# Load durations in the planner, the staging depth of the weights, and a rule of order for float32 matmuls

## The chip, the cores and the metric

The kernel runs on one core of a Trainium2 chip. The metric is the device time of one execution in microseconds, as the median of several runs. PE (TensorE) multiplies matrices, DVE (VectorE), ACT (ScalarE) and POOL (GpSimd) work element by element, SP (SyncE) issues the DMAs here. Each engine works through its own instructions in the written order.

## The reference

A dynamic convolution is followed by two feed-forward layers. There are 8192 tokens of 192 features.

```python
# 1. convolution: softmax over 7 taps for each token and each of 8 heads, then a weighted sum
w = exp(weight_gen - max); w = w / (sum(w) + 1e-9)
x = einsum('bshk,bskhg->bshg', w, last_7_tokens(x))      # (8192, 192)
# 2. a layer with a rational activation, 192 -> 2048 -> 192
h = x @ w_in
P = a0 + a1*h + a2*h**2 + a3*h**3
Q = 1 + abs(b0)*abs(h) + abs(b1)*h**2
x = (P / (Q + 1e-6)) @ w_out
# 3. a layer with hard swish, 192 -> 2048 -> 192
h = x @ w_in2
out = (h * clip(h + 3, 0, 6) / 6) @ w_out2
```

The four weight matrices come as float64 (x and the gate weights as float32), 12.6 MB in all, so the kernel decodes their bit patterns to float32 itself.

## The kernel before

**Tiling.** The tokens are cut into 32 blocks of 256 (a block is also a unit, `u`). The first layer works a block in four slots (`sl`), each with 4 of the 16 groups of 128 hidden features: 1024 columns. So there are 128 slots. The convolution loads x and the gate weights in 16 chunks (`load_chunk`, two units each, 945 to 960 KB of x and 112 KB of gate weights).

**First layer, per slot.** in1 (PE, L281) makes h in one of two PSUM buffers `h1`; for accuracy each product is five float32r matmuls of 256 columns, with weights and x split in a high and a low part. The activation then goes back and forth between ACT (L310 to L353), POOL (L329, L366, L377) and DVE (L333, L337, L358, L370) and ends in `ghi` and `glo`. `dve_d` (L370) is the last reader of `h1`, so in1 of a slot waits for dve_d of the slot two before. out1 (PE, L397 to L401) adds the slot to `y1`, of which there is one buffer.

**Second layer, per unit.** mid_y, mid_f and the steps around them turn y1 into the next input. in2 (L281 with win1, eight steps `q`), act_r2 (L419) and dve_g2 (L424) make g; out2 (L438, four parts of 16 matmuls in full float32, 128x192) makes the output, and evac stores it. The xT transposes (L206, L207) and mid_f (L250) are full float32 as well; all other matmuls are float32r.

**Weights.** 28 jobs load a piece of a weight each: "in" pieces of 512 KB, "pair" pieces (two halves, 512 KB together), "o1" and "o2" pieces of 384 KB. SP loads the float64 words to a staging tile `st` (ring of ST tiles), ACT decodes (`low` L490 and `scale` L484), DVE joins (L496) and sets the sign (L503), which frees the staging tile; then ACT makes the high part (L510) and POOL the low one (L511). The second layer's tiles are in memory that is free only after all jobs (`late`).

**Order.** The order on every engine is written by a planner at build time, `plan()`. Each operation has an engine, a cost, a due time `prio`, operations that it comes after, and rings of buffers that it takes from. The planner repeatedly picks the operation with the smallest rank: the earliest time at which it could start, plus a penalty for the choice of engine, plus KP times what its due time is ahead of the oldest open one's by more than WIN; ties go to the earlier due time. The multiplies of the convolution (L171) and the low parts (L511) may go to POOL or, with a handicap in us (CP and PEN), to DVE. So a cost that is wrong in the plan changes no instruction, but their order. Due times of the first layer grow by T for each slot; the constants from CH to UM set the offsets, LP how much earlier a job's load is due than its decode, XQ the same for a chunk.

SP's queue in the start, by the due times: pair 0, chunk 0, "in" piece 0, the coefficients, chunk 1, then the other jobs in their order. The planner counts 1.46 us for a 512 KB load, three quarters of that for 384 KB, and 3.1 us for a chunk, and 2.2 us more until the data is there.

Of the kernel before, what the change touches and what calls it, by code (L numbers as in the profile page):

```python
# [19 lines left out]
def kernel(  # L20
# [28 lines left out]
    BV = [n // 2 for n in BL]  # L49
# [52 lines left out]
    wgt = {}  # L102
    wk = {}

    def load_chunk(c):
        g = two.tile([P, CT * H, K], F32, tag="wg", name="wg")
        nc.sync.dma_start(
            out=g.rearrange("p (t h) k -> p t (h k)", h=H), in_=wgf[:, c * CT : (c + 1) * CT, :]
        )
        t = two.tile([P, ROWS, D], F32, tag="x", name="x")  # L110
        first = c * CT - (K - 1)
        neg = max(0, -first)
        segs = [(0, P)]
        if neg:
            segs = [(b * S // R + 1, (b + 1) * S // R) for b in range(B)]
            for b in range(B):
                p = b * S // R
                nc.gpsimd.memset(t[p : p + 1, 0:neg, :], 0.0)
                nc.sync.dma_start(
                    out=t[p : p + 1, neg:, :], in_=xf[None, b * S : b * S + ROWS - neg, :]  # L120
                )
        for p0, p1 in segs:
            src = bass.AP(
                tensor=xf.tensor,
                offset=xf.offset + (first + p0 * R) * D,
                ap=[[R * D, p1 - p0], [1, ROWS * D]],
            )
            nc.sync.dma_start(out=t[p0:p1].rearrange("p r d -> p (r d)"), in_=src)
        xch[c] = t
        wgt[c] = g  # L130

    def softmax_a(c):
        g = wgt[c]
# [313 lines left out]
        nc.sync.dma_start(out=of[:, u * 2 : u * 2 + 2, :], in_=o)  # L447

    CW = 512
    ST = 4  # L450

    def load_rows(dst, src):
        srcs = src if isinstance(src, list) else [src]
# [127 lines left out]
                    l(eng)  # L581

    G2 = 11
    T = 9.094
    CH = 5.027
    KP = 0.221
    XP = 17
    LP = 43.011
    LOADP = {(0, "load"): -100.0, (1, "load"): -80.0}
    WIN = 29  # L590
    PEN = 1.976
    CP = 3
    JP0 = 0.189
    JPT = 1.514
    HOLD = 6
    URG = 4.005
    UR = 17.898
    UG = 15.269
    SM = 1.345
    CV = 3.0  # L600
    XTP = 2.0
    XQ = 7.596
    I2 = 2.702
    SPR = 0.483
    O2 = 3.176
    OS = 3.771
    O1 = 1.491
    UM = 1.45
    ops = {}

    def op(key, eng, cost, prio, emit, after=(), take=(), lat=0.15):
# [5 lines left out]
    def add(name, eng, cost, prio, fn, *a, after=(), take=(), lat=0.15):  # L617
        op((name,) + a, eng, cost, prio, lambda *e: fn(*a, *e), after, take, lat)
# [9 lines left out]
    for n, key in enumerate(order):  # L628
# [10 lines left out]
            )  # L639

        flex = (("POOL", 1.25 * sz, 0.0), ("DVE", 0.62 * sz, PEN))
        step("load", "SP", 1.46 * sz, None, [("st", ST, [("job", key, "sign")])] if f64 else wf, 2.2)
        if f64:
            step("low", "ACT", 0.55 * sz, "load")
            step("scale", "ACT", 0.55 * sz, "load", [("s", NSB, [("job", key, "sign")])])
# [8 lines left out]
    TU = [S0[b] * T - (4 * (BV[b] - 1 - v) + XTP) * T for b, v in UB]  # L654
    for c in range(NCH):
        t = TU[2 * c] - CV * T + 1.9
        add("load", "SP", 3.1, t - XQ * T if c else -90.0, load_chunk, c, lat=2.2, take=[
            ("x", 2, [("conv_mul", 2 * c + 1, 1)]), ("wg", 2, [("softmax_b", c)]),
        ])
        add("softmax_a", "DVE", 0.75, t - SM * T + 2.85, softmax_a, c, after=[("load", c)])  # L660
        add("softmax_e", "ACT", 0.28, t - SM * T + 4.1, softmax_e, c, after=[("softmax_a", c)])
        add("softmax_b", "DVE", 1.5, t - SM * T + T + 6.6, softmax_b, c, after=[("softmax_e", c)],
            take=[("wk", 2, [("conv_mul", 2 * c + 1, 1)])])
    for u, (b, v) in enumerate(UB):
        t = TU[u]
        for i in range(2):
            flex = (("POOL", 2.6, 0.0), ("DVE", 1.6, CP))
            add("conv_mul", flex, 0, t + (2 * i - CV) * T + 1.9, conv_mul, u, i,
                after=[("load", u // 2), ("softmax_b", u // 2)],
                take=[("prod", 1, [("conv_sum", u, i, 1)])])  # L670
            for z in range(2):
                prev = [("conv_sum", u, i, 0)] if z else [("conv_sum", u, 0, 1)] if i else []
                add("conv_sum", "DVE", 1.33, t + (2 * i + z + 1 - CV) * T + 1.9, conv_sum, u, i, z,
                    after=[("conv_mul", u, i)] + prev,
                    take=[("xc", 2, [("xT", u)])] if i + z == 0 else [])
# [6 lines left out]
    for b in range(len(BL)):  # L682
        sl = S0[b] + NF // BF[b] - 1
        t = (sl + 2) * T
# [66 lines left out]
    def coeffs():  # L751
# [4 lines left out]
    op(("bab",), "ACT", 0.2, -1.0,  # L756
       lambda: nc.scalar.activation(out=bab, in_=bcol, func=AF.Abs), [("coeffs",)])

    def plan():
        free = {e: 0.0 for e in ("PE", "ACT", "DVE", "POOL", "SP")}  # L760
        end, rings, users, wait = {}, {}, {}, {}
# [15 lines left out]
        for o in sorted(ops.values(), key=lambda o: -o["prio"]):  # L777
            for f, *_ in o["choice"]:
                todo[f].append(o)
        seq = []  # L780
        while len(seq) < len(ops):
            best = None
            for e, rs in ready.items():
# [4 lines left out]
                for o, cost, pen in rs:  # L788
                    at = max([free[e]] + [end[k] for k in o["after"]])
                    for name, depth, _ in o["take"]:  # L790
# [4 lines left out]
                        if len(ring) >= depth:  # L795
                            for k in ring[-depth]:
                                at = max(at, end.get(k, float("inf")))
                    rank = (at + pen + KP * max(0.0, o["prio"] - cur - WIN), o["prio"])
                    if at < float("inf") and (pick is None or rank < pick[:2]):
                        pick = (*rank, at, e, cost, o)  # L800
# [2 lines left out]
            _, _, at, e, cost, o = best  # L803
            for f, *c in o["choice"]:
                ready[f].remove((o, *c))
            free[e] = at + cost
            end[o["key"]] = at + cost + o["lat"]
            for name, depth, rel in o["take"]:
# [53 lines left out]
```

## Time and profile before

| what | value |
|---|---|
| median of 3 runs | 1397.72 us (1397.65 to 1398.44) |
| the profiled execution, its own time | 1398.85 us |
| its span, first to last instruction | 1397.0 us |
| mean granted TensorE clock | 0.986 |
| PE busy | 1300.9 us, 93% |
| DVE, ACT, POOL busy | 1109.3, 1052.6, 1105.4 us |
| DMA queue q1 | 15656 packets, 36.44 MB |

Busy shares are of the whole span. Matmuls are pipelined and their ends modelled, so matmul times are best read from start to start. In a row of a timeline, xN means that N like instructions are merged, and the bracket says how long the engine was idle before it and what ended that.

### The profile page before, as it was taken

The numbers are of one execution on the slowest core, as the hardware profiler recorded it, in microseconds if no ns is written. First come the engines' busy times: TensorE is split into PE (matmuls) and PEld (weight loads), VectorE is DVE, ScalarE is ACT, GpSimd is POOL, SyncE is SP. The second block draws the span as 40 slices with busy tenths as digits, with TensorE's granted clock in tenths as the row PEclk, the third lists the DMA queues.
The fourth block names the chain that finished last, engine by engine and source line by source line (L and its number), as shares of the span: only waits on it lengthen the run. The fifth ranks groups of instructions, "written<-read, shape, count | busy, mean of one in ns | idle before, by whom it ended". The sixth has DMA issues, their size and how long they took to land.

```text
span 1397.0 us, 24025 instructions
## 1 busy us (share of the span) xinstructions
PE 1300.9 (93%) x9920; PEld 1292.0 (92%) x9920; DVE 1109.3 (79%) x1144; ACT 1052.6 (75%) x1326; POOL 1105.4 (79%) x492
## 2 busy tenths in 40 slices
PE   0468999999999999999999999999999999999998
PEld 0458999999999999999999999999999999999998
DVE  4988878788787878878788887878888787887762
ACT  4898777777877777787777778777778877777871
POOL 4898888878788887878878787887878888788670
PEclk9789999999999999999999999999999999999999
DMA  7530010000101000010100001010010100000000
GB/s 186 156 117 30 7 38 6 11 29 7 38 7 38 7 10 29 7 38 7 39 7 7 33 7 38 7 38 7 1 38 7 38 7 7 7 0 7 7 7 12
DMA packets 15765, 37.97 MB, mean 27 GB/s; under 512 B 1832, under 2 KB 12072, under 8 KB 15656
## 3 DMA queue, kind: packets, MB, share of 16 engines
q1 hardware_dynamic: 15656, 36.44, 8.4%
q8 instruction: 78, 1.28, 0.4%
q14 instruction: 31, 0.25, 0.1%
HBM read 30.14 MB, written 6.29 MB: 26 GB/s over the span
## 4 chain that ended last, share of the span: by engine, by line
PE 82%; DVE 6%; ACT 4%; issue 3%; DMA 2%; POOL 2%; SPq 0%; DVEq 0%; POOLq 0%
PE h L281 38%; PE y L438 24%; PE y L400 4%; PE y L401 4%; PE y L398 4%; PE y L399 4%; PE y L397 4%; DVE xc L186 2%; DMA st<-in_moe_w_in_dram 2%; DVE w L370 1%; DVE ghi L358 1%; ACT r L349 1%; ACT r L344 1%; PE yf L250 1%; DMA acol<-in_moe_a_dram 1%
## 5 line engine op out<-in xcount | busy, mean ns | idle before, releaser
L366 POOL TENSOR_TENSOR w<-w,ghi 128x1024 f32<-128x1024 f32 x128 | 308.0, 2406 | 162.4 <-DVE ghi L358 162.3
L438 PE MATMUL y<-wo,g 128*128 128x192 f32 x2048 | 353.4, 326 | 0.0
L329 POOL TENSOR_TENSOR w<-w,u 128x1024 f32<-128x1024 f32 x128 | 308.4, 2410 | 38.8 <-ACT w L315 38.5
L377 POOL TENSOR_TENSOR glo<-w,r 128x1024 fp32r<-128x1024 f32 x128 | 308.0, 2406 | 33.3 <-DVE w L370 18.0
L438 PEld LDWEIGHTS y<-wo,g 128*128 128x128 f32 x2048 | 331.1, 190 | 0.0
L281 PE MATMUL h<-xh,wst 128*128 128x256 f32 x1024 | 292.6, 286 | 0.0
L281 PE MATMUL h<-xl,wst 128*128 128x256 f32 x1024 | 292.3, 285 | 0.1
L358 DVE SCALAR_TENSOR_TENSOR ghi<-h,acol,r 128x1024 fp32r<-128x1024 f32 x128 | 163.7, 1279 | 103.5 <-ACT r L349 103.4
L344 ACT ACTIVATE r<-w 128x1024 f32<-128x1024 f32 x128 | 135.1, 1056 | 117.0 <-POOL w L329 116.7
L419 ACT ACTIVATE r<-h 128x512 f32<-128x512 f32 x256 | 153.3, 599 | 89.3 <-PE h L281 75.8
L333 DVE TENSOR_TENSOR l<-h,l 128x1024 f32<-128x1024 f32 x128 | 156.4, 1222 | 65.3 <-ACT l L322 64.8
L281 PE MATMUL h<-xh,win0hi 128*128 128x256 f32 x512 | 159.1, 311 | 48.5 <-DVE w L370 47.8
L281 PEld LDWEIGHTS h<-xl,wst 128*128 128x128 f32 x1024 | 199.2, 194 | 0.3 <-DVE xl L264 0.3
L281 PEld LDWEIGHTS h<-xh,wst 128*128 128x128 f32 x1024 | 199.0, 194 | 0.1
L424 DVE SCALAR_TENSOR_TENSOR g<-r,h 128x512 f32<-128x512 f32 x256 | 171.6, 680 | 24.6 <-ACT r L419 24.6
L186 DVE TENSOR_REDUCE xc<-prod 128x96 f32<-128x672 f32 x128 | 174.4, 1372 | 20.6 <-POOL prod L171 20.6
L370 DVE SCALAR_TENSOR_TENSOR w<-h,acol,w 128x1024 f32<-128x1024 f32 x128 | 163.7, 1279 | 22.5 <-POOL w L366 20.4
L310 ACT ACTIVATE u<-h 128x1024 f32<-128x1024 f32 x128 | 130.7, 1021 | 53.0 <-PE h L281 52.6
L171 POOL TENSOR_TENSOR prod<-x,wk 128x1344 f32<-128x1344 f32 x64 | 158.1, 2470 | 11.6 <-DVE wk L150 8.0
L337 DVE SCALAR_TENSOR_TENSOR h<-l,acol,h 128x1024 f32<-128x1024 f32 x128 | 164.1, 1282 | 0.1
L315 ACT ACTIVATE w<-u,bab 128x1024 f32<-128x1024 f32 x128 | 159.3, 1244 | 0.0
L397 PE MATMUL y<-ghi,wo1h 128*128 128x256 f32 x512 | 156.1, 305 | 0.0
(71 smaller groups left out, 3256.1 us busy)
## 6 DMA issues: line engine op xcount, KB each, us to landing
x<-in_x_dram SPq DMA_DIRECT2D x14, 960.0 KB, 4.7
st<-in_moe_w_out_dram SPq DMA_DIRECT2D x16, 384.0 KB, 3.6
out_dram<-osb SPq DMA_DIRECT2D x32, 192.0 KB, 1.9
st<-in_moe_w_in_dram SPq DMA_DIRECT2D x8, 512.0 KB, 10.7
st<-in_moe_w_in_dram SPq DMA_DIRECT2D x8, 256.0 KB, 4.7
x<-in_x_dram SPq DMA_DIRECT2D x4, 472.5 KB
wg<-in_weight_gen_dram SPq DMA_DIRECT2D x16, 112.0 KB, 2.7
x<-in_x_dram SPq DMA_DIRECT2D x2, 3.0 KB
```

The source lines that it names most:

```text
L186: nc.vector.tensor_reduce(out=xc[u][:, i, hs], in_=prod[u, i].rearrange("p k h g -> p (h g) k")[:, hs, :], axis=AX.X, op=ALU.add,)
L281: nc.tensor.matmul(out=dst, lhsT=l[:, fs], rhs=r, start=(n == 0), stop=(n == len(seq) - 1), skip_group_check=True,)
L315: nc.scalar.activation(out=w, in_=e1[sl]["u"], func=AF.Identity, scale=bab[:, 1:2], bias=bab[:, 0:1])
L329: nc.gpsimd.tensor_tensor(out=e["w"], in0=e["w"], in1=e["u"], op=ALU.mult)
L337: nc.vector.scalar_tensor_tensor(out=h, in0=e["l"], scalar=acol[:, 1:2], in1=h, op0=ALU.add, op1=ALU.mult)
L358: nc.vector.scalar_tensor_tensor(out=ghi, in0=h, scalar=acol[:, 0:1], in1=e["r"], op0=ALU.add, op1=ALU.mult)
L366: nc.gpsimd.tensor_tensor(out=m, in0=m, in1=g1[sl][0].bitcast(F32), op=ALU.mult)
L370: nc.vector.scalar_tensor_tensor(out=m, in0=h1.pop(sl), scalar=acol[:, 0:1], in1=m, op0=ALU.add, op1=ALU.subtract)
L377: nc.gpsimd.tensor_tensor(out=glo, in0=e["m"], in1=e["r"], op=ALU.mult)
L397: mm(out=a, lhsT=wo1h[:, n, :], rhs=gh, start=st, stop=False, **kw)
L424: nc.vector.scalar_tensor_tensor(out=fl(g), in0=r, scalar=1.0, in1=fl(h), op0=ALU.min, op1=ALU.mult,)
L438: nc.tensor.matmul(out=y2[u][:, s, :], lhsT=g[:, i, s * P : (s + 1) * P], rhs=wo2[:, n, :], start=(n == 0 and s == 0), stop=(n == NF - 1), ...
```

## The change

Five things are changed. The loads' costs in the plan become 2.85 us for 512 KB (and three quarters of it for 384 KB) and 5.3 us for a chunk of x, with 2.0 us more until the data is there; the gate weights' load is an operation of its own, `gen`, at 0.6 us. The staging ring has 8 tiles where it had 4. The due times of the first loads are set one by one, and most constants of the planner have new values (CP, the handicap of DVE for the convolution's multiplies, from 3 to 0.982; XTP, JPT and CP's partner PEN keep theirs or nearly so). While fewer than SWL us of full-float32 work have run in a row on PE, other PE operations get a penalty of 0.01 us. A `gate` can make the convolution's multiplies wait for in1 of a slot; it is empty as long as GATED is 0.

```diff
--- before.py
+++ after.py
@@ -102,11 +102,14 @@
     wgt = {}
     wk = {}
 
-    def load_chunk(c):
+    def load_gen(c):
         g = two.tile([P, CT * H, K], F32, tag="wg", name="wg")
         nc.sync.dma_start(
             out=g.rearrange("p (t h) k -> p t (h k)", h=H), in_=wgf[:, c * CT : (c + 1) * CT, :]
         )
+        wgt[c] = g
+
+    def load_chunk(c):
         t = two.tile([P, ROWS, D], F32, tag="x", name="x")
         first = c * CT - (K - 1)
         neg = max(0, -first)
@@ -127,7 +130,6 @@
             )
             nc.sync.dma_start(out=t[p0:p1].rearrange("p r d -> p (r d)"), in_=src)
         xch[c] = t
-        wgt[c] = g
 
     def softmax_a(c):
         g = wgt[c]
@@ -447,7 +449,7 @@
         nc.sync.dma_start(out=of[:, u * 2 : u * 2 + 2, :], in_=o)
 
     CW = 512
-    ST = 4
+    ST = 8
 
     def load_rows(dst, src):
         srcs = src if isinstance(src, list) else [src]
@@ -581,31 +583,37 @@
                     l(eng)
 
     G2 = 11
-    T = 9.094
-    CH = 5.027
-    KP = 0.221
+    T = 9.201
+    CH = 4.875
+    KP = 0.314
     XP = 17
-    LP = 43.011
-    LOADP = {(0, "load"): -100.0, (1, "load"): -80.0}
-    WIN = 29
-    PEN = 1.976
-    CP = 3
-    JP0 = 0.189
+    LP = 60
+    J0P = -88.058
+    J1P = -92.851
+    GATED = 0
+    SWL = 5.5
+    LEAD = 4.104
+    X0P = -112.382
+    LOADP = {(0, "load"): J0P, (1, "load"): J1P}
+    WIN = 19.0
+    PEN = 2
+    CP = 0.982
+    JP0 = -3.294
     JPT = 1.514
-    HOLD = 6
-    URG = 4.005
-    UR = 17.898
-    UG = 15.269
-    SM = 1.345
-    CV = 3.0
+    HOLD = 5.0
+    URG = 13.058
+    UR = 13.252
+    UG = 13.453
+    SM = 1.042
+    CV = 3.132
     XTP = 2.0
-    XQ = 7.596
-    I2 = 2.702
-    SPR = 0.483
-    O2 = 3.176
-    OS = 3.771
-    O1 = 1.491
-    UM = 1.45
+    XQ = 7.472
+    I2 = 6.483
+    SPR = 0.477
+    O2 = 8.383
+    OS = 2.187
+    O1 = 3.181
+    UM = 5.922
     ops = {}
 
     def op(key, eng, cost, prio, emit, after=(), take=(), lat=0.15):
@@ -639,7 +647,7 @@
             )
 
         flex = (("POOL", 1.25 * sz, 0.0), ("DVE", 0.62 * sz, PEN))
-        step("load", "SP", 1.46 * sz, None, [("st", ST, [("job", key, "sign")])] if f64 else wf, 2.2)
+        step("load", "SP", 2.85 * sz, None, [("st", ST, [("job", key, "sign")])] if f64 else wf, 2.0)
         if f64:
             step("low", "ACT", 0.55 * sz, "load")
             step("scale", "ACT", 0.55 * sz, "load", [("s", NSB, [("job", key, "sign")])])
@@ -654,19 +662,26 @@
     TU = [S0[b] * T - (4 * (BV[b] - 1 - v) + XTP) * T for b, v in UB]
     for c in range(NCH):
         t = TU[2 * c] - CV * T + 1.9
-        add("load", "SP", 3.1, t - XQ * T if c else -90.0, load_chunk, c, lat=2.2, take=[
-            ("x", 2, [("conv_mul", 2 * c + 1, 1)]), ("wg", 2, [("softmax_b", c)]),
-        ])
-        add("softmax_a", "DVE", 0.75, t - SM * T + 2.85, softmax_a, c, after=[("load", c)])
+        add("gen", "SP", 0.6, t - XQ * T if c else X0P, load_gen, c, lat=2.0,
+            take=[("wg", 2, [("softmax_b", c)])])
+        add("load", "SP", 5.3, t - XQ * T + 1.0 if c else X0P + 0.5, load_chunk, c, lat=2.0,
+            take=[("x", 2, [("conv_mul", 2 * c + 1, 1)])])
+        add("softmax_a", "DVE", 0.75, t - SM * T + 2.85, softmax_a, c, after=[("gen", c)])
         add("softmax_e", "ACT", 0.28, t - SM * T + 4.1, softmax_e, c, after=[("softmax_a", c)])
         add("softmax_b", "DVE", 1.5, t - SM * T + T + 6.6, softmax_b, c, after=[("softmax_e", c)],
             take=[("wk", 2, [("conv_mul", 2 * c + 1, 1)])])
+
+    def gate(u):
+        b, v = UB[u]
+        sl = S0[b] - 4 * (BV[b] - 1 - v) - int(LEAD)
+        return [("in1", sl, 1)] if 0 <= sl < GATED else []
+
     for u, (b, v) in enumerate(UB):
         t = TU[u]
         for i in range(2):
             flex = (("POOL", 2.6, 0.0), ("DVE", 1.6, CP))
             add("conv_mul", flex, 0, t + (2 * i - CV) * T + 1.9, conv_mul, u, i,
-                after=[("load", u // 2), ("softmax_b", u // 2)],
+                after=[("load", u // 2), ("softmax_b", u // 2)] + gate(u),
                 take=[("prod", 1, [("conv_sum", u, i, 1)])])
             for z in range(2):
                 prev = [("conv_sum", u, i, 0)] if z else [("conv_sum", u, 0, 1)] if i else []
@@ -756,6 +771,8 @@
     op(("bab",), "ACT", 0.2, -1.0,
        lambda: nc.scalar.activation(out=bab, in_=bcol, func=AF.Abs), [("coeffs",)])
 
+    FULL = ("out2", "xT", "mid_f")
+
     def plan():
         free = {e: 0.0 for e in ("PE", "ACT", "DVE", "POOL", "SP")}
         end, rings, users, wait = {}, {}, {}, {}
@@ -778,6 +795,7 @@
             for f, *_ in o["choice"]:
                 todo[f].append(o)
         seq = []
+        run = 0.0
         while len(seq) < len(ops):
             best = None
             for e, rs in ready.items():
@@ -795,6 +813,8 @@
                         if len(ring) >= depth:
                             for k in ring[-depth]:
                                 at = max(at, end.get(k, float("inf")))
+                    if e == "PE" and 0.0 < run < SWL and o["key"][0] not in FULL:
+                        pen = pen + 0.01
                     rank = (at + pen + KP * max(0.0, o["prio"] - cur - WIN), o["prio"])
                     if at < float("inf") and (pick is None or rank < pick[:2]):
                         pick = (*rank, at, e, cost, o)
@@ -803,6 +823,8 @@
             _, _, at, e, cost, o = best
             for f, *c in o["choice"]:
                 ready[f].remove((o, *c))
+            if e == "PE":
+                run = run + cost if o["key"][0] in FULL else 0.0
             free[e] = at + cost
             end[o["key"]] = at + cost + o["lat"]
             for name, depth, rel in o["take"]:
```

## Rows read from the trace of the kernel before

**Rows 1.** The page: busy us of each engine, share of the span, instructions.

```profile
PE 1300.9 (93%) x9920; PEld 1292.0 (92%) x9920; DVE 1109.3 (79%) x1144; ACT 1052.6 (75%) x1326; POOL 1105.4 (79%) x492
```

**Rows 2.** Stretches: us; busy (x) of PE, PEld, DVE, ACT, POOL; PEclk, DMA share, GB/s.

```profile
10.00:24.00 14.00, 0.00 (x0) 0.00 (x0) 5.62 (x8) 2.67 (x6) 7.84 (x5) 1.00 0.88 191
24.00:37.00 13.00, 2.04 (x6) 1.08 (x6) 10.09 (x16) 11.07 (x23) 5.95 (x4) 1.00 0.60 183
37.00:59.50 22.50, 6.64 (x39) 6.43 (x39) 21.05 (x24) 20.97 (x37) 16.88 (x16) 0.74 0.55 171
59.50:105.60 46.10, 29.13 (x164) 27.48 (x164) 39.76 (x52) 40.54 (x63) 44.50 (x29) 0.79 0.39 117
...
140.00:1371.00 1231.00, 1210.74 (x9341) 1206.55 (x9341) 994.30 (x1003) 939.46 (x1148) 997.54 (x417) 1.00 0.05 17
```

**Rows 3.** Waits, 140 to 1360 us: total us, times, longest us.

```profile
PE h L281 <- DVE w L370: 20.3, 13, 1.6
```

**Rows 4.** Timeline of POOL: start us, us, instruction [idle before <-releaser].

```profile
9.13 2.59 POOL L511 TENSOR_TENSOR wst<-wf,wst 64x512 fp32r<-64x512 f32 x2 [4.17 <-ACT wst L510]
12.85 2.46 POOL L171 TENSOR_TENSOR prod<-x,wk 128x1344 f32<-128x1344 f32 x1 [1.13 <-DVE wk L150]
...
19.15 2.46 POOL L171 TENSOR_TENSOR prod<-x,wk 128x1344 f32<-128x1344 f32 x1 [0.55 <-DVE xc L186]
```

**Rows 5.** Timeline of DVE, in the start.

```profile
16.51 2.50 DVE L186 TENSOR_REDUCE xc<-prod 128x96 f32<-128x672 f32 x2
25.86 0.70 DVE L496 SCALAR_TENSOR_TENSOR dt<-dt,st 128x512 int32<-128x512 int32 x1 [6.86 <-ACT dt L484]
...
30.26 1.33 DVE L186 TENSOR_REDUCE xc<-prod 128x96 f32<-128x672 f32 x1
...
32.10 1.29 DVE L186 TENSOR_REDUCE xc<-prod 128x96 f32<-128x672 f32 x1
...
34.24 1.00 DVE L503 SCALAR_TENSOR_TENSOR wf<-st,dt 128x384 int32<-128x384 int32 x2
...
105.05 0.55 DVE L503 SCALAR_TENSOR_TENSOR wo<-st,dt 128x384 int32<-128x384 int32 x1
```

**Rows 6.** Timeline of ACT, in the start.

```profile
5.77 0.65 ACT L490 ACTIVATE st<-st 128x512 int32<-128x512 uint32 x1 [3.75 <-DMA st<-in_moe_w_in_dram]
...
24.67 0.67 ACT L490 ACTIVATE st<-st 128x512 int32<-128x512 uint32 x1 [7.41 <-DMA st<-in_moe_w_in_dram]
...
34.18 0.31 ACT L200 ACTIVATE xc<-xc 128x128 f32<-128x128 f32 x1
```

**Rows 7.** Timeline of SP's DMA issues, in the start.

```profile
0.74 1.19 SPq L456 DMA_DIRECT2D st<-in_moe_w_in_dram  x2
...
9.51 3.02 SPq L128 DMA_DIRECT2D x<-in_x_dram  x2
...
16.66 11.10 SPq L456 DMA_DIRECT2D st<-in_moe_w_out_dram  x2
```

**Rows 8.** Timeline of PE, in the start.

```profile
36.90 0.58 PE L281 MATMUL h<-xl,win0hi 128*128 128x256 f32 x1 [0.18 <-DVE xl L222]
```

**Rows 9.** Timeline of PE, around sixteen out2 matmuls, and the last unit's sixty-four.

```profile
302.30 0.28 PE L401 MATMUL y<-glo,wo1s 128*128 128x256 f32 x1
302.42 2.77 PE L438 MATMUL y<-wo,g 128*128 128x192 f32 x16
...
305.14 0.28 PE L398 MATMUL y<-ghi,wo1l 128*128 128x256 f32 x1
...
1383.18 10.56 PE L438 MATMUL y<-wo,g 128*128 128x192 f32 x64
```

**Rows 10.** Sources L136 and L171: durations ns min/median/max, first and last start.

```profile
L136 DVE TENSOR_TENSOR wg<-wg,mx x16: 392/2485/2494, 8.7 to 1191.0; 128x224 f32<-128x224 f32 x16
L171 POOL TENSOR_TENSOR prod<-x,wk x64: 2456/2468/2486, 12.8 to 1260.0; 128x1344 f32<-128x1344 f32 x64
```

**Rows 11.** Timeline of PE, at one wait of the steady part.

```profile
377.99 0.38 PE L281 MATMUL h<-xh,win0hi 128*128 128x256 f32 x1 [1.56 <-DVE w L370]
```

## The prediction

> **What bounds the kernel now.** I read the page's busy times first. PE is busy 93% of the span, with every other engine at 75 to 79% [rows 1]. That is an average over two very different stretches, so the table of stretches comes next. From 140 to 1371 us PE is busy 1210.74 of 1231.00 us; up to 105.6 us it is busy 2.04 + 6.64 + 29.13 = 37.8 us [rows 2]. So this is a program bound by PE with a slow start, and whatever moves the start moves the end one for one, since the work behind it is fixed.
>
> What is left to gain after 140 us is what the view of the waits shows there: PE's matmuls of L281 (in1) wait 20.3 us in 13 waits for DVE L370 [rows 3]. L370 is `dve_d`, the last reader of an `h1` buffer; there are two of those, so in1 of a slot needs dve_d of the slot two before. 20.3 is all of the idle time of the stretch (1231.00 - 1210.74).
>
> In the start the timelines of the engines, read together, say why in1 first runs at 36.9 us [rows 4 to 8]. The x chunk for it landed early enough for POOL to multiply at 12.85 [rows 4], and the second multiply is over at 19.15 + 2.46 = 21.6. Yet the sums that follow on DVE run only at 30.26 and 32.10: ahead of them in DVE's queue stand the joins of weight pieces, the first of which starts at 25.86 after 6.86 us of idleness [rows 5], because ACT's decode of that piece waited 7.41 us for its DMA [rows 6]. The planner believed that this piece would land early (1.46 us for a load); in truth SP had put chunk 1 (two transfers that it issues from 9.51 to 12.53) in front of it [rows 7]. An engine works in the written order, so a wrong duration in the plan becomes a wait in the run.
>
> **Part by part. Loads with true durations, and the order of the first loads.** SP's first loads become: gate weights 0, x chunk 0, "in" piece 0, pair 0, coefficients, then the jobs in their order; chunk 1 (due -40.5 and -39.5 by the new constants) goes behind about 14 further job loads, whose due times are -63.3 + 1.514n, instead of in front of them. The DMA engines move 191 GB/s while there is enough in flight [rows 2]. Gate weights and chunk 0 are 112 + 945 KB, 1.08 MB, 5.7 us. The first 512 KB in the old order were ready for ACT at 5.77 [rows 6]; 2.75 us of that are their bytes at 191 GB/s, 0.74 is SP's first issue [rows 7], so about 2.3 is latency. Chunk 0 is then there at 0.74 + 5.7 + 2.3 = 8.7; I take 9.5, since "in" piece 0 flies beside it. Then "in" piece 0 at 11.5 and pair 0 at 14.3 (2.75 us each).
>
> From there the chain of chunk 0, by the durations of before: multiply 2.46 [rows 4], two sums 2.50, multiply 2.46, two sums 1.33 + 1.29 [rows 5], and from x_dup's start at 34.18 [rows 6] to the matmul at 36.90 [rows 8] 2.72 us: 12.8 us in all. A join and a sign of two pieces come between on DVE, of which I count 1.4 us as in the way (they fit partly under POOL's multiplies). 9.5 + 12.8 + 1.4 = 23.7 against 36.9: **-13.2 us**. Bounds: -15.4 with nothing in between (8.7 + 12.8 = 21.5); -7 if the last sums again stand behind a decode, that of the fifth piece, landing at 22.6 (22.6 + 2 for ACT and DVE + 2.62 + 2.72 = 29.9). The weights aren't late: pair 0 had its low part on POOL done at 9.13 + 2.59, 6 us after it was there [rows 4], which would be 20.3.
>
> Something is owed for that. When in1 began, 7 pieces were decoded (the double sign at 34.24 is the sixth and seventh [rows 5]); by 23.7 us the DMA has delivered five, and four and a half are decoded. The missing 2.5 pieces at about 1.8 us of ACT each (three instructions near the 0.67 of the one at 24.67 [rows 6], shorter for an "out" piece) are done later, beside slots. Between 24 and 105.6 us ACT is busy 72.6 of 81.6 us, DVE 70.9 and POOL 67.3 [rows 2], so nearly all of it shows: **+4 us** (0 to +5).
>
> **Eight staging tiles.** With four, a load waits for the sign of the fourth job before: SP issued two of the "out" pieces over 11.1 us from 16.66 [rows 7], and the DMA engines' share falls from 0.88 to 0.60, 0.55 and 0.39 in the stretches that follow [rows 2]. The last piece is signed at 105.05 + 0.55 = 105.6 [rows 5], and stage 2 waits for it (`late`). By bytes alone, 12.6 MB of weights and 2.2 MB of chunks 0 and 1 take 78 us at 191 GB/s, so that the last piece could be decoded at about 84. But the decode, not the transfer, is then the bound: the three engines above are 82 to 89% busy, and no instruction of theirs goes away. What better order can return is part of ACT's 9 idle us in that stretch. I take **-3 us** (0 to -9). Chunk 1, moved back, lands at about 53 us (9.5 MB in front and with it). It serves slots 8 to 15, and eight slots of some 10 us (1231 us for about 120 of them) come first, so its move costs nothing; only some 30 us later would it hold slot 8.
>
> **Float32 matmuls together.** While fewer than 5.5 us of out2, xT or mid_f have run in a row, others rank 0.01 us behind; up to three out2 can then follow one another. The gain is what a return to float32r costs. 16 matmuls of out2 cost (10.56 - 2.77) / 48 = 0.162 us each [rows 9], 2.60 us together; the float32r matmul after them 0.12, the step from 302.30 to 302.42. The row of L398 behind it starts 305.14 - 302.42 = 2.72 us after the first of the sixteen [rows 9], which is the same. **0** (at most 0.01 for each of some 150 such runs: 0 to -1.5).
>
> **The rest.** The gate weights' own load is the same DMA as before under its own name, and the gate on conv_mul is empty, as GATED is 0: both 0. The new due times change each engine's order in the steady part. The nearest row is the present stall, 20.3 us in 13; I take it that one like it remains, **0**, with -20.3 below, and above it the price of rival C. The tail is the last unit's own chain and keeps its instructions: 0 (2 either way).
>
> Sum: -13.2 + 4 - 3 = -12.2. The profiled execution took 1398.85 us around a span of 1397.0; 1398.85 - 12.2 = 1386.65. The median of the runs lies 1.13 us under it, which gives **1385.5 us**.
>
> **Rivals.** *A: the steady stall goes too.* For it: the wait comes at one place of a pattern that repeats with the chunks (13 waits, 16 chunks). There softmax_a's L136 takes 2.485 us, where its shortest is 0.392 [rows 10], PE then waits 1.56 us [rows 11], and the softmax is what the new constants move. Against: nothing in the change tells the planner that L136 can take 2.5 us; its cost for softmax_a is still 0.75. Time: 1385.5 - 20.3 = 1365.
>
> *B: the start's gain is hidden.* For it: ACT, DVE and POOL at 82 to 89% from 24 to 105.6 us; if the plan there is no denser, what is gained at the first in1 is owed in decode and comes back at the last sign, 105.6. Against: ACT is busy just 2.67 of the 14 us from 10 to 24 [rows 2], time that earlier pieces can fill. Left over: some 2.5 us; 1395.
>
> *C, slower: multiplies of the convolution on DVE.* CP, the handicap of DVE for conv_mul, falls from 3 to 0.98. Before, all 64 ran on POOL [rows 10], in 2.5 us each: waiting for one such instruction was always cheaper than 3. At 0.98 a wait of over 1 us tips it, and POOL is busy 81% of the steady part [rows 2] with instructions of about that length; I estimate 16 to 32 of 64. On DVE one is planned at 1.6 us. But L136, the same kind (two inputs from SBUF), grows by 2.09 us, and that is what makes PE wait 1.56 at 377.99 [rows 10, 11]. If each such multiply costs PE a wait like that, 8 of them eat the 12.2 us; 20 cost 31 and give 1385.5 + 31 = 1416. Against: DVE is idle 19% of the steady part, and a delayed multiply is needed only much later.
>
> The Trainium skill, page "SBUF — State Buffer", section "Who interferes with whom", says that a VectorE instruction with two SBUF inputs contends with a GpSimd instruction that reads SBUF, over a shared port; L136's 0.39 and 2.49 us agree. By that rule a multiply moved to DVE gains no overlap with POOL, which speaks for C.
>
> **How the numbers follow.** The forecast has 0.43, its own range 1378 to 1393 (the bounds of the start's three terms, not all at one end). A 0.20, B 0.13, C 0.24. The range 1364 to 1410 takes in A and B and the lower part of C, and leaves out a fifth. 0.2% or 2.8 us is about what a measurement of this kernel can tell from no change. Faster: the forecast nearly whole, A, and half of B, 0.68. Slower: most of C and a rest of the forecast, 0.23. Within: 0.09.
>
> **What would show it.** First in1 with both operands at 22 to 26 us, DVE's sums of chunk 0 directly behind POOL's multiplies; the last sign before 98; no long issue wait of SP before 30 us; the busy PE of the steady part unchanged at about 1210 for the same matmuls. Rival C would show as L171 on DVE with durations of 2 to 4 us, and more than 13 waits of L281 for L370. The prediction is wrong if the first in1 is early and the last sign still falls at 105 (B), or if the steady part's idle time leaves 10 to 30 us.

## The result, and the profile after

The changed kernel takes **1376.02 us** (median of 4 runs, 1375.60 to 1376.24) against 1398.08 us beside it: a ratio of 0.984 (95% interval 0.9823 to 0.9857), or 22.1 us less. Forecast were 1385.5 us, 12.2 us less, with 1378 to 1393 us as the forecast's own range and 1364 to 1410 us as the range that takes in rivals.

The page's first part again, then the stretches (us; busy and instructions of PE, PEld, DVE, ACT, POOL; PEclk, DMA share, GB/s), to be held against [rows 1, 2].

```profile
PE 1303.9 (95%) x9920; PEld 1291.6 (94%) x9920; DVE 1091.2 (79%) x1144; ACT 1041.6 (76%) x1326; POOL 1102.1 (80%) x492
```

```profile
10.00:24.00 14.00, 1.10 (x4) 0.68 (x4) 8.58 (x10) 6.46 (x12) 8.42 (x5) 1.00 1.05 228
24.00:37.00 13.00, 6.90 (x42) 6.15 (x40) 10.89 (x13) 10.91 (x18) 8.95 (x6) 0.93 0.51 172
37.00:59.50 22.50, 7.54 (x40) 7.07 (x40) 16.73 (x25) 21.79 (x41) 21.29 (x21) 0.65 0.66 200
59.50:105.60 46.10, 26.37 (x133) 24.26 (x134) 40.70 (x53) 41.49 (x67) 41.24 (x26) 0.71 0.31 98
...
0.00:140.00 140.00, 75.52 (x478) 71.07 (x479) 109.55 (x134) 109.60 (x170) 112.38 (x78) 0.84 0.43 122
140.00:1340.00 1200.00, 1198.25 (x9236) 1190.95 (x9235) 973.99 (x999) 925.24 (x1145) 986.79 (x414) 1.00 0.05 17
```

Before, the last two stretches read:

```profile
0.00:140.00 140.00, 67.97 (x429) 64.33 (x430) 108.70 (x132) 106.59 (x166) 107.90 (x76) 0.87 0.43 122
140.00:1340.00 1200.00, 1179.74 (x9106) 1175.55 (x9106) 976.81 (x985) 921.48 (x1126) 978.34 (x409) 1.00 0.05 17
```

A matmul takes 0.130 us on the average here (1198.25 us for 9236 of them), so the counts of PE say where the time came from. Up to 140 us there are 478 - 429 = 49 more, 6.4 us of work done earlier; from 140 to 1340 us there are 9236 - 9106 = 130 more, 16.9 us. The two make 23.3 us, and the spans differ by 1397.0 - 1373.8 = 23.2. So only a quarter of the gain lies in the start, where all of it had been forecast.

**The start.** First the timelines of POOL, DVE, ACT, PE and SP, which answer to [rows 4 to 8].

```profile
12.14 2.46 POOL L173 TENSOR_TENSOR prod<-x,wk 128x1344 f32<-128x1344 f32 x1 [8.06 <-DMA bcol<-in_moe_b_dram]
17.89 2.46 POOL L173 TENSOR_TENSOR prod<-x,wk 128x1344 f32<-128x1344 f32 x1 [3.29 <-DVE xc L188]
```

```profile
14.63 1.28 DVE L188 TENSOR_REDUCE xc<-prod 128x96 f32<-128x672 f32 x1 [8.98 <-POOL prod L173]
...
16.43 1.31 DVE L188 TENSOR_REDUCE xc<-prod 128x96 f32<-128x672 f32 x1
...
20.38 2.58 DVE L188 TENSOR_REDUCE xc<-prod 128x96 f32<-128x672 f32 x2 [0.71 <-POOL prod L173]
...
97.82 0.55 DVE L505 SCALAR_TENSOR_TENSOR wo<-st,dt 128x384 int32<-128x384 int32 x1
```

```profile
13.55 0.66 ACT L492 ACTIVATE st<-st 128x512 int32<-128x512 uint32 x1 [9.49 <-DMA st<-in_moe_w_in_dram]
...
22.99 0.31 ACT L202 ACTIVATE xc<-xc 128x128 f32<-128x128 f32 x1
```

```profile
25.66 0.58 PE L283 MATMUL h<-xl,win0hi 128*128 128x256 f32 x1
```

```profile
5.43 8.59 SPq L458 DMA_DIRECT2D st<-in_moe_w_in_dram  x4
14.95 2.07 SPq L458 DMA_DIRECT2D st<-in_moe_w_out_dram  x2
```

The sums now follow the multiplies, and no decode that waits for its data stands in front of them. in1 has both operands at 25.66 us, 11.2 us earlier. But POOL's first multiply runs at 12.14, after 8.06 us of idleness that a DMA ended; chunk 0 had been put at 9.5. (The bracket names `bcol`, which this instruction does not read; what it takes from a DMA is x, whose landing the trace does not hold.) SP still takes 8.59 us for four issues from 5.43, where no long wait was forecast. And the last sign falls at 97.82 + 0.55 = 98.4, 7.2 us earlier, not the 11.2 of in1.

**The steady part.** The view of the waits for PE, from 140 to 1340 us (us, times, longest), answers to [rows 3]:

```profile
PEld h L283 <- DVE w L372: 2.5, 13, 0.2
PE h L283 <- DVE g L426: 1.5, 2, 0.7
```

20.3 us of waits for dve_d (L370, now L372) have become a loading of weights that is 0.2 us late 13 times. The sources of the two instructions of [rows 10] under their new lines:

```profile
L138 DVE TENSOR_TENSOR wg<-wg,mx x16: 393/2428/2432, 3.2 to 1176.5; 128x224 f32<-128x224 f32 x16
L173 POOL TENSOR_TENSOR prod<-x,wk x64: 2459/2468/2499, 12.1 to 1246.5; 128x1344 f32<-128x1344 f32 x64
```

L138 still takes 2.43 us, against 0.39 at its first start: what made dve_d late is still there, and no longer reaches PE. One place of the pattern shows why, on DVE and PE:

```profile
372.49 2.43 DVE L138 TENSOR_TENSOR wg<-wg,mx 128x224 f32<-128x224 f32 x1
375.97 1.27 DVE L372 SCALAR_TENSOR_TENSOR w<-h,acol,w 128x1024 f32<-128x1024 f32 x1
```

```profile
372.04 5.37 PE L440 MATMUL y<-wo,g 128*128 128x192 f32 x32
377.30 0.39 PE L283 MATMUL h<-xh,win0hi 128*128 128x256 f32 x1
```

in1 still starts 0.06 us after the end of dve_d (375.97 + 1.27 = 377.24), as it did before: there dve_d ran from 376.66 to 377.94 and in1 from 377.99 [rows 11]. But now two out2 parts in a row give PE work until then; before, PE had nothing for 1.56 us. It is the same for all 13 of the L138 that take 2.43 us. And all 64 multiplies are on POOL as before, in spite of CP.

### The profile page after: what moved, and what is told of

Its sections match the earlier page's. It is cut to its first block, busy times and chain, and to the rows that moved or that the text cites. A ratio compares the mean times of both kernels' runs of the same rounds, so it can differ in the third digit from the quotient of the medians.

```text
span 1373.8 us, 23974 instructions
## 1 busy us (share of the span) xinstructions
PE 1303.9 (95%) x9920; PEld 1291.6 (94%) x9920; DVE 1091.2 (79%) x1144; ACT 1041.6 (76%) x1326; POOL 1102.1 (80%) x492
## 4 chain that ended last, share of the span: by engine, by line
PE 91%; ACT 3%; POOL 3%; DVE 1%; issue 1%; DMA 1%; SPq 0%; POOLq 0%; DVEq 0%; ACTq 0%
PE h L283 43%; PE y L440 24%; PE y L402 4%; PE y L403 4%; PE y L400 4%; PE y L399 4%; PE y L401 4%; PE yf L252 1%; DMA bcol<-in_moe_b_dram 1%; POOL prod L173 1%; POOL glo L379 1%; PE xT L209 1%; PE xT L208 0%; POOL w L331 0%; ACT l L324 0%
## 5 line engine op out<-in xcount | busy, mean ns | idle before, releaser
L440 PE MATMUL y<-wo,g 128*128 128x192 f32 x2048 | 348.3, 326 | 0.0
L372 DVE SCALAR_TENSOR_TENSOR w<-h,acol,w 128x1024 f32<-128x1024 f32 x128 | 163.4, 1277 | 74.8 <-POOL w L368 74.8
L421 ACT ACTIVATE r<-h 128x512 f32<-128x512 f32 x256 | 150.1, 594 | 83.5 <-PE h L283 67.9
L173 POOL TENSOR_TENSOR prod<-x,wk 128x1344 f32<-128x1344 f32 x64 | 158.2, 2472 | 32.4 <-DVE wk L152 16.9
L324 ACT ACTIVATE l<-h,acol 128x1024 f32<-128x1024 f32 x128 | 153.9, 1202 | 1.2 <-PE h L283 1.2
```

The source lines that it names most:

```text
L173: eng.tensor_tensor(out=pr, in0=xch[c][:, t : t + K, :].rearrange("p k (h g) -> p k h g", g=G), in1=wk[c][:, :, t * H : (t + 1) * H, None] ...
L372: nc.vector.scalar_tensor_tensor(out=m, in0=h1.pop(sl), scalar=acol[:, 0:1], in1=m, op0=ALU.add, op1=ALU.subtract)
L440: nc.tensor.matmul(out=y2[u][:, s, :], lhsT=g[:, i, s * P : (s + 1) * P], rhs=wo2[:, n, :], start=(n == 0 and s == 0), stop=(n == NF - 1), ...
```

## The experiments

| kernel | us | ratio to before (95%) | PE matmuls, 0 to 140 | 140 to 1340 us |
|---|---|---|---|---|
| before | 1398.1 to 1398.6 | 1 | 429 | 9106 |
| changed | 1376.0 | 0.984 (0.9823 to 0.9857) | 478 | 9236 |
| loads8 | 1391.0 | 0.9947 (0.9933 to 0.9962) | 475 | 9130 |
| loads4 | 1391.4 | 0.9947 (0.9932 to 0.9962) | 482 | 9116 |
| nogroup | 1391.3 | 0.995 (0.9935 to 0.9965) | 478 | 9140 |
| group | 1544.0 | 1.1042 (1.1023 to 1.106) | | 8140 |
| group_nomax | 1541.8, one run | | | 8133 |
| group_late | 1401.0, one run | | | 9088 |
| nomax | 1374.4 | 0.9829 (0.9814 to 0.9843) | | 9291 |
| softcost | 1384.6 | 0.9903 (0.9889 to 0.9918) | | 9222 |
| after_nolow | 1374.2 | 0.983 (0.9814 to 0.9847) | 491 | |
| after_rowmax | 1362.4 | 0.974 (0.9723 to 0.9756) | | 9319 |
| after_pad | 1365.8 | 0.978 (0.9757 to 0.9802) | | 9286 |
| rowmax_same | 1374.0 | 0.9825 (0.981 to 0.984) | | 9251 |

### Which part of the change gives what

**loads8.** The kernel before with the part on loads:

```diff
-    LP = 43.011
-    LOADP = {(0, "load"): -100.0, (1, "load"): -80.0}
-    ST = 4
+    LP = 60
+    X0P = -112.382
+    LOADP = {(0, "load"): -88.058, (1, "load"): -92.851}
+    ST = 8
...
+    # costs 2.85 and 5.3, latency 2.0, gen apart: as in the change
```

> The kernel before with everything of the change that concerns loads (true durations, the gate weights' load by itself, due times of the first loads, LP 60, eight staging tiles), all other constants old and no rule for float32 matmuls. Theory 1 (the loads give the start's 6 us and nothing else; the steady part's 16 us come from elsewhere): about 1392 us, first in1 near 25 us, and L281 still waits for L370 about 20 us after 140 us. Theory 2 (the whole gain hangs on the loads, since a plan that starts differently also falls into another steady pattern): about 1376, the steady waits gone.

1391.0 us: theory 1. The waits of the steady part stay as they were:

```profile
PE h L283 <- DVE w L372: 18.6, 12, 1.6
```

The loads give 7.3 us, most of it in the start: 475 matmuls up to 140 us against 429, 6.0 us of work.

**loads4.** The same with `ST = 4`.

> loads8 (1391 us) with four staging tiles in place of eight: true durations and new order of the first loads alone. Theory (the order of DVE's queue was the fault, and the ring of four costs little once the durations are true): 1390 to 1393. Rival (eight tiles carry the gain, since with four the DMA engines stand still behind signs): 1395 to 1399, first in1 near 25 us all the same but the last sign at 105.

1391.4 us, the same as with eight; in1 has both operands at 25.29. SP does wait longer for the ring: four issues take it 13.76 us and two take 5.02, where the rows of the changed kernel above have 8.59 and 2.07. It makes no difference to the time:

```profile
5.29 13.76 SPq L458 DMA_DIRECT2D st<-in_moe_w_in_dram  x4
19.27 5.02 SPq L458 DMA_DIRECT2D st<-in_moe_w_out_dram  x2
```

So the staging tiles are worth nothing here (0.4 us, within the spread of the runs), and the rest of the loads' part is the whole of the 7 us: the durations in the plan, the due times of the first loads with LP, and `gen`. Which of these gives how much was not tried.

**group.** The kernel before with the rule for float32 matmuls alone:

```diff
+                    if e == "PE" and 0.0 < run < SWL and o["key"][0] not in FULL:
+                        pen = pen + 0.01
...
+            if e == "PE":
+                run = run + cost if o["key"][0] in FULL else 0.0
```

> The kernel before with nothing but the rule that keeps out2, xT and mid_f together (0.01 us, up to 5.5 us). Theory 3 (the rule is what removes the steady wait, since in1 then has longer work of PE ahead of it and is asked for later): about 1378 to 1382 us, runs of float32 matmuls from 159 to about 80, waits of L281 for L370 after 140 us under 5 us. Rival (the new due times remove it): 1398 within 3 us, the waits stay near 20 us.

1544.0 us: 10% slower, which neither theory had. The waits of PE in the steady part, then PE's and ACT's timeline at one of them:

```profile
PE yf L250 <- ACT ys L229: 64.3, 12, 5.4
PE h L281 <- DVE w L370: 14.2, 14, 1.3
```

```profile
237.73 0.28 PE L401 MATMUL y<-glo,wo1s 128*128 128x256 f32 x1
243.37 1.22 PE L250 MATMUL yf<-ys,fold 128*128 128x256 f32 x2 [5.36 <-ACT ys L229]
```

```profile
238.06 1.06 ACT L344 ACTIVATE r<-w 128x1024 f32<-128x1024 f32 x1 [2.42 <-POOL w L329]
...
241.82 1.23 ACT L315 ACTIVATE w<-u,bab 128x1024 f32<-128x1024 f32 x1
242.95 0.37 ACT L229 ACTIVATE ys<-y 128x256 f32<-128x256 f32 x1
```

mid_f (L250) needs `ys` from ACT, which needs the last out1 of the block. That out1 starts at 237.73; ACT takes five instructions of the activation first and makes `ys` at 242.95; mid_f stands next in PE's queue. In the kernel before, the last out1 of a block starts at 395.78, ACT makes `ys` 0.6 us later, and an out2 part lies between the out1 and mid_f (ACT's row, then PE's):

```profile
396.41 0.38 ACT L229 ACTIVATE ys<-y 128x256 f32<-128x256 f32 x1
```

```profile
395.90 2.77 PE L438 MATMUL y<-wo,g 128*128 128x192 f32 x16
398.50 0.59 PE L250 MATMUL yf<-ys,fold 128*128 128x256 f32 x2
```

So two things differ: with the rule ACT comes to `ys` 5.2 us after that out1 in place of 0.6, and PE has nothing left to do meanwhile, since the unit's four out2 parts had all run by 228.1 us. Which of the two the harm needs was not separated. In every second unit of group twenty matmuls of in1 lie between, ACT makes `ys` after 1.1 us, and mid_f does not wait.

The wait costs more than itself. PE's last out1 was over at 238.0; at 242.07, while PE was still idle, the granted clock fell to 0.50 (1.2 GHz), and it rose again at 248.90. The pair of mid_f matmuls takes 1.22 us in that stretch and 0.59 in the kernel before. Each of the 12 waits has such a stretch, and the mean from 140 to 1340 us is 0.97 where it was 1.00:

```profile
242.07:248.90 6.83, 5.53 (x22) 5.05 (x23) 3.57 (x6) 3.56 (x7) 6.22 (x3) 0.50 0.00 0
140.00:1340.00 1200.00, 1105.24 (x8140) 1083.64 (x8138) 892.40 (x892) 817.15 (x1004) 870.23 (x366) 0.97 0.05 16
```

PE is 9106 - 8140 = 966 matmuls behind the kernel before, some 126 us. The idle time is 1200 - 1105.24 = 94.8 us, 74.5 more than before. Twelve stretches with 5.53 us of work at half the clock cost about 33 us, an estimate from the first row above; the rest was not followed up.

**nogroup.** The changed kernel with `SWL = 0.0`.

> The changed kernel with the rule switched off (SWL 0), all else new. Theory 3 (the rule removes the steady wait): 1388 to 1396 us, PE idle by 10 us or more from 140 to 1346 us. Rival (the new due times do): 1376 within 3 us.

1391.3 us: the rule is worth 15.3 us in the changed kernel. Against loads8 (1391.0) the new due times alone are worth nothing. The long waits are gone without the rule already, but 36 short ones have come:

```profile
140.00:1340.00 1200.00, 1192.27 (x9140) 1180.39 (x9139) 955.52 (x990) 918.13 (x1133) 976.87 (x410) 1.00 0.05 17
...
PE h L283 <- DVE w L372: 7.2, 36, 0.9
```

The idle time is 1200 - 1192.27 = 7.7 us, 6.0 more than in the changed kernel, and less than the 10 us expected; by the count, 9140 matmuls against 9236, PE is 12.5 us behind. The difference lies in how the view counts: a row of a float32r matmul lasts 0.28 us, though the next one can start 0.12 us after it, so the first 0.16 us of a wait do not show as idle. Read from start to start, matmuls begin later than their usual step by 20.0 us in sum here (the delays over 0.03 us, 140 to 1340 us) and by 6.4 us in the changed kernel: 13.6 us, and nearly all of it at in1, for dve_d.

So the gain belongs to the rule and the other parts together: 0 for the new due times and constants beside the loads' part, 146 us lost for the rule in the kernel before, 15 gained for the rule in the changed one. The due times without the loads' part, and the rule with the loads' part alone, were not run.

**group_late.** group with out2 due as in the changed kernel:

```diff
-    O2 = 3.176
-    OS = 3.771
+    O2 = 12.164
+    OS = 2.187
```

> group (1544 us) with the due times of out2 alone put where the changed kernel has them (O2 12.164, OS 2.187 by the old I2). Theory (the rule used up the four out2 parts of a unit early, and nothing of PE's was left to cover the wait of mid_f for ACT's ys; out2 due later leaves one or two): under 1420 us, waits of mid_f for ys under 15 us. Rival (out2's place is not the point; mid_y and in2 have to move too): over 1480, the waits near 64 us.

1401.0 us: two constants take back 143 of the 146 us, and no wait of mid_f for ACT is left; the old one for dve_d is back:

```profile
PE h L281 <- DVE w L370: 21.2, 13, 1.6
```

(O2 counts from I2, and 12.164 + 2.702 is the 8.383 + 6.483 of the change.) That the rule's harm hangs on when out2 is due is shown. How is not, and the theory's reason does not fit: in this trace no out2 part lies between the last out1 and mid_f but ten matmuls of in1, and ACT makes `ys` 0.3 us after the start of that out1. With these two constants alone the rule also hardly acts: there are 159 runs of full-float32 matmuls, as many as before, against 130 in group and 81 in the changed kernel.

### What made PE wait before

**nomax.** The kernel before, without L135 and L136 for chunks 2 to 15:

```diff
-        nc.vector.tensor_reduce(out=mx, in_=g, axis=AX.X, op=ALU.max)
-        nc.vector.tensor_tensor(
-            out=g, in0=g, in1=mx[:, :, None].to_broadcast([P, CT * H, K]), op=ALU.subtract
-        )
+        # for c < 2 alone
```

> The kernel before, where the softmax of chunks 2 to 15 leaves out the subtraction of the maximum (L135 and L136), nothing else. Theory (L136, held up by POOL to 2.49 us, is what delays dve_d and makes PE wait 1.56 us once a chunk): the waits of L281 for L370 after 140 us fall from 20 us to under 4, the time to about 1380. Rival (dve_d is late there for its order behind the sums and g2, and L136 only fills time that POOL's L366 sets): the waits stay above 14 us and the time above 1390.

1374.4 us: 24 us less, a little more than the waits of 20.3, and PE is busy without a pause (read from start to start, the matmuls of the kernel before are late by 23.7 us in sum, those of nomax by 0.1):

```profile
140.00:1340.00 1200.00, 1200.00 (x9291) 1198.45 (x9290) 957.17 (x975) 935.93 (x1147) 992.44 (x416) 1.00 0.05 17
```

So without L135 (0.38 us) and L136 (2.49 us) in 14 chunks the whole of the steady part's idle time is gone. That L136 lasts so long because of POOL is what its place says. In the kernel before, DVE's row and POOL's at the wait of [rows 11]:

```profile
372.36 2.49 DVE L136 TENSOR_TENSOR wg<-wg,mx 128x224 f32<-128x224 f32 x1
```

```profile
372.17 2.42 POOL L366 TENSOR_TENSOR w<-w,ghi 128x1024 f32<-128x1024 f32 x1 [2.22 <-DVE ghi L358]
```

L136 starts 0.19 us behind L366 and ends 0.26 us after it (374.85 against 374.59), the same in all 14 places; at 8.7 us, with POOL idle, it takes 0.39. The Trainium skill, page "SBUF — State Buffer", section "Who interferes with whom", has the same: two inputs from SBUF contend with GpSimd's reads. The 0.39 and 2.49 us of the traces here agree.

**softcost.** The kernel before, `softmax_a` planned at 2.9 us where it was 0.75.

> The kernel before with one number changed in the plan: softmax_a costs 2.9 us on DVE (the measured 0.38 + 2.49) where it cost 0.75. Theory (the steady wait is a planning error like that of the loads: where the plan knows the length, it puts dve_d ahead of the softmax): 1376 to 1384 us, waits of L281 for L370 after 140 us under 5 us. Rival (the greedy plan takes what can start first and does not look ahead, so that dve_d stands behind the softmax all the same): 1394 to 1400, the waits near 20 us.

1384.6 us, 14 us less from one number in the plan, just above the theory's range. The waits for dve_d are gone but for one; smaller ones for POOL's last step took their place:

```profile
PE y L400 <- POOL glo L377: 4.6, 13, 0.4
...
PE h L281 <- DVE w L370: 1.0, 1, 1.0
```

The plan did not put dve_d ahead of the softmax, as the theory had it, but right behind L136 (371.61 to 374.08 in this trace), in front of the sum and the g2 that stood between them before:

```profile
374.00 1.27 DVE L370 SCALAR_TENSOR_TENSOR w<-h,acol,w 128x1024 f32<-128x1024 f32 x1
```

So the wait came from L136 and from what followed it in DVE's queue; taking either away ends it.

**group_nomax.** group and nomax together.

> The rule for float32 matmuls with the old constants, as in group (1544 us), and the softmax of chunks 2 to 15 without the subtraction of its maximum, as in nomax. Theory (the rule's harm is a cascade: the plan leaves no slack, the 2 us that POOL's lock adds to L136 make mid_y late and PE waits 5.5 us for it): 1375 to 1400 us, the waits of mid_f for ACT's ys nearly gone. Rival (with the old due times the rule itself asks for an order in which ACT, DVE and POOL can't keep up): over 1480 us, the waits of mid_f for ys stay.

1541.8 us, the waits of mid_f at 64.3 us as in group. My theory of a cascade from L136 fell; the rule's harm hangs on the due times of out2 (group_late).

### Where 5 us of the start went

**after_nolow.** The changed kernel without ACT's decode of the low words:

```diff
-        nc.scalar.activation(
-            out=low, in_=low.bitcast(U32), func=AF.Copy, scale=0.936 * 2.0 ** -29
-        )
+        return
...
-            out=yi, in0=yi, scalar=3, in1=j["st"][:, :, 0],
+            out=yi, in0=yi, scalar=3, in1=j["st"][:, :, 1],
```

> The changed kernel without the ACT instruction that decodes the low word of the weights (L492, 28 instructions of 0.55 to 0.67 us; DVE's join takes the high word in its place, so the weights are other values), the plan and all else as it is. Theory (the start after the first in1 is bound by decode on ACT, which is where 5 of the 11 us gained at the first in1 went): 1366 to 1372 us, last sign at 88 to 94 instead of 98.4. Rival (it is bound by the chain of each slot through in1, the activation and dve_d, in which the decode only fills gaps): 1374 to 1378, last sign within 2 us of 98.

1374.2 us, 1.9 us less, and the last sign at 96.5. The stretch from 24 to 105.6 us, changed kernel first:

```profile
24.00:105.60 81.60, 40.81 (x215) 37.48 (x214) 68.33 (x89) 74.18 (x124) 71.49 (x51) 0.73 0.44 138
```

```profile
24.00:105.60 81.60, 43.08 (x221) 39.73 (x221) 69.46 (x90) 63.10 (x100) 70.98 (x51) 0.73 0.46 136
```

ACT has 74.18 - 63.10 = 11.1 us less to do, and 1.9 of it come out at the end. The rival is nearer: the decode on ACT is not what bounds the start. What does was not shown. In the changed kernel's trace the chain of work that ended last goes, from 24 to 107 us, over ACT and POOL in about equal parts (31 and 29 us). The granted clock is another candidate that no run separates: its mean is 0.65 and 0.71 in the stretches from 37 and from 59.5 us, 0.74 and 0.79 before [rows 2].

### A version that beats both, and why

**after_rowmax.** One maximum for all 32 groups of a partition, subtracted by the exponential:

```diff
-        mx = two.tile([P, CT * H], F32, tag="mx", name="mx")
-        nc.vector.tensor_reduce(out=mx, in_=g, axis=AX.X, op=ALU.max)
-        nc.vector.tensor_tensor(...)
+        mx = nmx[c] = two.tile([P, 1], F32, tag="nmx", name="nmx")
+        nc.vector.tensor_reduce(
+            out=mx, in_=g.rearrange("p t k -> p (t k)"), axis=AX.X, op=ALU.max, negate=True
+        )
...
+        nc.scalar.activation(out=wgt[c], in_=wgt[c], func=AF.Exp, bias=nmx.pop(c)[:, 0:1])
```

> The changed kernel, whose softmax subtracts the maximum over all 32 groups of a partition (one reduction, then the bias of the exponential) in place of each group's own: the same result by the softmax's invariance, and L138 with its two inputs from SBUF is gone. Theory (in the changed kernel PE no longer waits for what L138 delays; it is idle just 1.75 us from 140 to 1346): 1373 to 1377 us. Rival (some of the steady part's remaining loss, and of the start's, still hangs on the lock): 1364 to 1371 us.

1362.4 us, 13.6 under the changed kernel and below the range of theory and rival, though PE had only 1.75 us of idle time left to give there. Two more kernels took it apart.

**after_pad.** The changed kernel with an unused tile:

```diff
+        two.tile([P, 1], F32, tag="nmx", name="nmx")
         nc.vector.tensor_reduce(out=mx, in_=g, axis=AX.X, op=ALU.max)
```

> The changed kernel with its softmax as it is and one unused tile of 4 bytes a partition (two buffers) added where after_rowmax has its own, so that the tiles behind it in that pool lie at other addresses. after_rowmax was 13.6 us faster than the changed kernel, and in its trace the float32r matmuls start every 117.7 ns where they start every 120.0 in all kernels before. Theory (the matmuls' spacing hangs on where tiles lie): 1361 to 1367 us, spacing near 118. Rival (it is the missing L138 and the lighter DVE): 1374 to 1378, spacing 120.

**rowmax_same.** after_rowmax with the maximum in the old tile `mx[:, 0:1]`.

> after_rowmax with its one maximum in the first column of the tile that was there before, so that no address changes against the changed kernel. Theory (addresses set the spacing): 1372 to 1377 us, spacing 120. Rival (the missing L138 sets it): 1361 to 1365, spacing near 118.

1365.8 us for the unused tile, 1374.0 us for the missing subtraction. The same 189 float32r matmuls in a row, first and last, in the changed kernel and in after_pad:

```profile
510.16 0.28 PE L283 MATMUL h<-xl,win0hi 128*128 128x256 f32 x1
...
532.72 0.28 PE L403 MATMUL y<-glo,wo1s 128*128 128x256 f32 x1
```

```profile
513.47 0.28 PE L284 MATMUL h<-xl,win0hi 128*128 128x256 f32 x1
...
535.70 0.28 PE L404 MATMUL y<-glo,wo1s 128*128 128x256 f32 x1
```

22.56 us against 22.23, over 188 steps: 120.0 and 118.3 ns. It is no matter of one row: over the float32r matmuls that follow one another from 140 to 1340 us (steps under 160 ns) the mean is 118.3 ns in after_pad and after_rowmax, and 119.8 to 120.0 in every other kernel of the table. 1.7 ns on each of the 7680 float32r matmuls (240 for each of 32 blocks) is 13 us, somewhat over the 10.2 us gained; read from start to start, the matmuls of after_pad's steady part are late by 11.2 us in sum against 6.4 in the changed kernel, which takes some of it back.

The four runs of after_pad took 1372.19, 1365.94, 1365.50 and 1365.66 us, and the trace is of the first. There the start is behind: 446 matmuls up to 140 us against 478 in the changed kernel, with the granted clock at 0.50 (1.2 GHz) from 138.71 to 145.54 us. The 10.2 us are from the median of the four.

So the unused tile sets the spacing, not the softmax. All that it changes in the kernel is where the tiles behind it lie; the addresses themselves were not read, and which tile, and which property of its address, was not tried.

## Why the prediction was right, and where it was not

The time lay inside the wide range and the sign was right, but 2 us below the forecast's own range of 1378 to 1393. Of the 22 us only the loads' 7.3 came from where the sum had put them; the other 15 came from a term put at 0. That the total still fell into the wide range is owed to rival A, whose size it nearly has, and not to the sum. By a sign that the prediction itself gave ("or if the steady part's idle time leaves 10 to 30 us") its mechanism was wrong: that idle time fell from 20.3 to 1.75 us.

- **The first in1.** Forecast -13.2, measured -11.2. The chain was right (13.5 us from multiply to in1 against 14.2), the start of it was not: chunk 0 was there at 12.1 us, not 9.5.
- **What is owed.** Forecast +4, measured 11.2 - 6.4 = 4.8 by the matmuls up to 140 us. The size was right, by luck, since the reason was wrong: I put it down to ACT's decode, and taking 11.1 us of that away gave back 1.9 (after_nolow). What it is stays open.
- **Eight tiles, -3.** Failed: 1391.0 with eight (loads8), 1391.4 with four (loads4). A queue's waits were read as a cost though the time does not hang on them. So the loads' part comes to -7.3 (loads8), where the start's three terms had -12.2.
- **Float32 matmuls together, 0.** This step failed most. "The gain is what a return to float32r costs" priced the switch, which is indeed free, and left out that a rule which breaks ties reorders PE's whole queue, and with it the other engines'. It is worth 15.3 us in the changed kernel and costs 146 in the kernel before.
- **The rest, 0.** The new due times, added to the loads' part, are 0 (nogroup against loads8). "I take it that one like it remains" failed all the same: with the rule the waits for dve_d went.
- **Rival A** came true in its size (16.9 us of the steady part against 20.3). The argument against it, that the plan still has the wrong cost for the softmax, was true and did not matter: L138 is nearly as long as before (2.43 us), and the new order has 32 rows of out2 in front of in1. That the softmax's maximum was the cause before is shown by nomax, and that the order behind it on DVE was as needed by softcost.
- **Rival B** is half true: of 11.2 us 6.4 are left. **Rival C** did not happen: no multiply went to DVE. The estimate of 16 to 32 multiplies had no row for how often DVE is free 1 us sooner than POOL in the plan.

## What to carry to other kernels

Look for the unplanned delay behind a repeated wait, and ask of every rule of order what work covers which wait, and what comes later on the other engines: a rule that gains 15 us with one set of constants loses 146 with another. Price a change of a planner not by the instructions that it touches but by the waits that its order exposes. And where a plan is built on costs, measure them beside the other engines: one number for one step, 0.75 made 2.9, was worth 14 us.

## What the hardware showed that I had not expected

- The spacing of float32r matmuls of 256 columns changed with an unused tile of 4 bytes a partition: 120.0 ns in the changed kernel, 118.3 in after_pad. That it is the address of some tile is the likely reason, not a shown one. It is worth 10.2 us (1376.0 to 1365.8).
- A return from full float32 to float32r costs PE nothing that its rows show: 2.72 us for sixteen and one [rows 9]. (An out2 part is 8 matmuls in the code and 16 rows in the trace: each full-float32 matmul stands there twice, at 0.162 us.)
- A wait of 5.4 us on PE is paid more than once: with PE idle since 238.0 us the granted clock fell at 242.07 to 0.50 (1.2 GHz), and it was back at 1.00 at 248.90, 5.5 us after the wait. The pair of mid_f matmuls behind it took 1.22 us, against 0.59 without such a wait.
